# A fused attention and GLU kernel on one Trainium2 core: down and output projections of three blocks with the weights stationary

## The chip, the core and the metric

The kernel runs on one core of one Trainium2 chip. The core has a matrix engine (TensorE, PE in the profile; its weight loads are listed apart as PEld), three engines for elementwise work (VectorE or DVE, ScalarE or ACT, GpSimd or POOL) and DMA engines. SyncE (SP) issues most transfers; POOL issues those that accumulate. Every engine works through its own list of instructions in order, and waits at semaphores for the others. The metric is the time of one execution on the device in microseconds (us); less is better.

## What is computed

The input x has 2048 tokens of 640 features, in bf16. It is normalized over the features, and two branches read the result xn. The output is x plus both.

```python
xn = _layernorm(x)
# A: 32 heads of 20 features; each token sees 8 keys, at distances 0, 2, ..., 14
q, k, v = split(xn @ wqkv)
attn = softmax(mask(einsum("bhsd,bhswd->bhsw", q, kg) * scale))
A = einsum("bhsw,bhswd->bhsd", attn, vg) @ wo            # 640 -> 640
# B: gated linear unit, no activation function
h = (xn @ w_gate) * (xn @ w_up)                           # 640 -> 1536
B = h @ w_down                                            # 1536 -> 640
return x + A + B
```

## The kernel before

**Tiling.** The tokens are cut into 16 tiles of 128 and into 4 blocks (j = 0 to 3) of 512. Features lie in chunks of 128: 5 chunks (`NCH`) of the 640, 12 chunks (`NF`) of the 1536. PSUM has 8 banks of 128 x 512 fp32.

**A planner sets the order.** `Sched` (from L40) is no part of the chip's work. While the program is built, generators hand it tasks, each for one engine, with what it reads and writes, a priority (less is earlier), a number of PSUM banks and a `slack` by which it is thought to be ready later. The planner keeps a clock for each engine, advanced by the assumed cost of an instruction (`occ`; for an accumulating transfer `acc`), and emits the task that can start first. What it writes is one fixed list for each engine, with semaphore waits at every dependency. On the chip a list is never reordered: where an engine comes to an instruction whose input is late, it waits, and all that is behind it waits too.

**The stages.**
- `front(t)`: statistics, normalization and transposition of a tile into XNT (features on partitions). The first tiles are transposed on PE and copied out of PSUM; tiles 0 and 1 in two parts, chunks 0 and 1 and then 2 to 4, each on the engine that `COPY` names (L503; copies at L653 and L655). From tile 4 on a transposing transfer does it (L675, on SP's queue). PE runs 18 idle matmuls (`warm`, L680, L1531) before the first tile.
- `proj_qk`, `proj_v` (matmuls at L698 and L730): q, k and v.
- `products` and `logits`: products of q with shifted k on DVE (L880, L929). For blocks 2 and 3 (`QUAD`) fp32 products of five feature chunks are summed pairwise by POOL (L955, L966, L988) or by accumulating transfers that POOL issues (L951; `BY_DMA`). The sum of the fifth chunk (`name + "c"`, L966) is on POOL everywhere, since `LAST_DMA` is empty. PE sums over the features of a head with the matrix G (L1012).
- `softmax` (DVE and ACT), then `weighted`: 20 units u = 5j + c. In each, DVE multiplies the shifted values with the weights (L1191), POOL adds two halves (two adds a unit, L1196), and `sums` lets PE add up the rest with the matrix SEL (L1250), in batches of units that `BATCH` lists. ACT copies the batch into OT (L1259).
- `gu`: for block j and hidden chunk m, gate and up products on PE (L1314), ACT copies the gate, DVE multiplies with the up product (L1323), giving h. The pairs in `FAST` have up copied by ACT first, so that DVE multiplies from SBUF (L1361); such a multiply and a POOL operation exclude each other in the planner (`lock`).
- `dn(j)` with `dn_piece`: the down product and the output product accumulate into one bank. **Tokens are stationary**: for each of 4 token tiles and 2 halves of 320 features, 12 matmuls with `ht[:, rows]` as weights and WD as moving operand, then 5 with OT and WO (L1416, 320 columns each). The first 12 may be done ahead; the last 5 need OT, that is, the batch of `sums`. For j < 3 ACT copies the result to FB0 (L703), token tile by token tile, and after all eight POOL issues one transfer that adds FB0 to the output in HBM (L1442), where x was copied before. For j = 3 DVE adds x and SP stores.

**Banks around the end.** Two banks hold the softmax weights for `weighted`, each batch of `sums` wants a bank per unit at once, and a down product started before OT is there must leave that many free (`keep=next_sums`).

Of the kernel before, what the change touches and what calls it, by code (L numbers as in the profile page):

```python
# [49 lines left out]
class Sched:  # L50
# [78 lines left out]
    def op(self, eng, fn, r=(), w=(), dma=False, name="", occ=None, lat=None, lock=False, nbytes=0, mode=0, group=None, extra=0.0, acc=0.0, land=None):  # L129
# [19 lines left out]
        if dma:  # L149
            self.t[eng] = start + (0.48 if occ is None else occ)  # L150
            if acc:
                self.t_acc = max(self.t_acc, start + 3.8) + acc
                X.end = self.t_acc
            else:
                self.t_data = max(self.t_data, start + 1.2) + nbytes / 280e3
                X.end = self.t_data + 0.8 + extra
            if land is not None:
                X.end, self.t_data = land, max(land - 0.8, self.t_data - nbytes / 280e3)
        else:
            self.t[eng] = start + occ  # L160
            X.end = start + (occ if lat is None else lat)
# [194 lines left out]
def build_kernel(nc, A_x, A_wqkv, A_wo, B_x, B_w_gate, B_w_up, B_w_down, out):  # L356
# [65 lines left out]
    PRD += [sb("PRD12", [128, 4, JB], at=a_sc), sb("PRD13", [128, 4, JB], at=a_sc + 4096)]  # L422
    PRD32 = [K.sbuf(f"PRF{i}", [128, 2, JB], FP32, K.base[p.name]) for i, p in enumerate(PRD)]
    QUAD = {2: (1, 0), 3: (1, 0)}
    LAST_DMA = ()
    BY_DMA = (((0, 0), (0, 2)), ((1, 0), (1, 2)))
    a_xr = place[0]
    FB0 = sb("FB0", [128, 5, D])
# [71 lines left out]
    op("pool", lambda e: e.memset(KT[:, :, 0:PAD], 0.0), w=[KT[:, :, 0:PAD]], name="kpad", occ=0.3)  # L500

    PARTS = (((0, 2), (2, NCH)), ((0, 2), (2, NCH)))
    COPY = (("act", "act"), ("act", "dve"))  # L503

    def part_of(t, c):
        return next(k for k, (lo, hi) in enumerate(PARTS[t]) if lo <= c < hi)
# [170 lines left out]
            yield Task("sp", dmat, r=[xs], prio=1)  # L677
        mark("xnt", t)

    def warm(n):  # L680
        for _ in range(n):
            op("pe", lambda e: e.matmul(PS[:, 7, 0:QB], ZERO[:, 0:128], ZERO[:, 0:QB], start=True, stop=True),
               r=[ZERO[:]], w=[PS[:, 7, :]], name="warm", occ=0.2 if n > 3 else 0.12)

    def wcols(which, c, m):
        if which == 2:
# [77 lines left out]
    def proj_qk():  # L764
        for pair in (0, 2):
            for which in (0, 1):
                for t in (pair, pair + 1):
                    yield have("xnt", t)
                    K.spawn(proj_group([(which, 0, 4 if pair else 5)], t * TS, TS, 10 if pair else FIRST + 0.5 * which + 0.2 * t, None))
            if pair:  # L770
                for which in (0, 1):
                    K.spawn(proj_group([(which, 4, 1)], pair * TS, 2 * TS, 10.2, None))
        for t in (4, 6):
            yield have("xnt", t + 1)
            for items in ([(0, 0, 2)], [(1, 0, 2)], [(0, 2, 2)], [(1, 2, 2)], [(0, 4, 1), (1, 4, 1)]):
                K.spawn(proj_group(items, t * TS, 2 * TS, 11 + t * 0.1, None))
        for j in (2, 3):
            yield have("xnt", 4 * j + 3)
            for m in range(NCH):
                for which in (0, 1):  # L780
                    if which or j not in QUAD or m == NCH - 1:
                        K.spawn(proj_group([(which, m, 1)], j * JB, JB, 12 + j, None))
# [61 lines left out]

    def products():
        rows = {j: [] for j in range(NJ)}
        joined = []
        holds = {}
        for at, (j, kind) in enumerate(ORDER):
            if kind == "w":  # L850
                if j not in holds:
                    yield from fetch(j, 0, holds.setdefault(j, {c: [] for c in range(4)}))
                yield from wide(j, rows[j], holds[j])
            else:
                if len(QUAD.get(j, ())) == 2 and j not in holds and (j, "w") == ORDER[at + 1]:
                    yield from fetch(j, 0, holds.setdefault(j, {c: [] for c in range(4)}))
                for r in (1, 0):
                    for c in range(NCH - 1 if r in QUAD.get(j, ()) else 0, NCH):
                        yield from narrow(j, r, c, rows[j])
            if len(rows[j]) == 10 - 4 * len(QUAD.get(j, ())) and kind == ("w" if j in QUAD else "n"):  # L860
                if j in JOIN:
                    joined.append((j, rows[j]))
                    if len(joined) == len(JOIN):
                        K.spawn(logits(*joined))
                else:
                    K.spawn(logits((j, rows[j])))
        mark("products")

    def narrow(j, r, c, slots):
# [40 lines left out]
    def wide(j, slots, hold):  # L910
        halves = [(r, q0) for r in QUAD[j] for q0 in (0, 2)]
        acc, parts = {}, {1: [], 0: []}
        lastc = {r: [n, 0] for n, _, r in slots}
        slots.clear()
        for c0 in (0, 2):
            for i, (r, q0) in enumerate(halves):
                f = []
# [29 lines left out]
    def sum32(j, r, q0, p, a, b, last=None):  # L947
        x, y = PRD32[a][:], PRD32[b][:]
        name = f"qsum{j}_{r}_{q0}_{p}"
        if (r, q0) in BY_DMA[p]:  # L950
            yield Task("pool", lambda: op("pool", lambda e: e.dma_start(x, y, accum_op=ALU.add), r=[x, y], w=[x], dma=True,  # L951
                                          name=name, occ=0.88, acc=3.4), r=[x, y], w=[x], prio=4)
        else:
            yield calm
            yield Task("pool", lambda: op("pool", lambda e: e.tensor_tensor(x, x, y, ALU.add), r=[x, y] + tokens(), w=[x],  # L955
                                          name=name, occ=2.36, lock=True), r=[x, y], w=[x], prio=5, lock=True)
        free.append(b)
        if last is None:
            return
        z = PRD[last[0]][:, q0:q0 + 2, :]  # L960
        if (r, q0) in LAST_DMA:
            yield Task("pool", lambda: op("pool", lambda e: e.dma_start(x, z, accum_op=ALU.add), r=[x, z], w=[x], dma=True,
                                          name=name + "c", occ=0.88, acc=3.4), r=[x, z], w=[x], prio=4)
# [138 lines left out]
        yield Task("sp", move, r=[L[:]], prio=4)  # L1102

    NU = NJ * NCH
    BATCH = (4, 9, 14, 17, 19)

    def vx_loads():
        yield have("products")
# [42 lines left out]
    def unit(u):  # L1151
# [1 line left out]
        if c == 0:  # L1153
            yield have("atx", j // 2)
        yield have("vx", u)
        for k, (ok, n) in enumerate(((("atx", 1) in done, (9,)), (count.get(("dn", 0), 0) >= 8, (5,)),
                                     (count.get(("dn", 1), 0) >= 8, (6, 7, 8)))):
            if ok and k not in more:
                more.append(k)
                sv_free.extend(n)  # L1160
# [76 lines left out]
    def sums(us):  # L1237
# [1 line left out]
        for u in us:  # L1239
            yield have("add", u)  # L1240
        if us[-1] >= 3 * NCH:
            yield num(8, "dn", 2)

        def go(*bs):
            hold.extend(bs)
# [15 lines left out]
                K.free_bank(b, X)  # L1261
                bump("ot", j)

        yield Task("pe", go, r=[SV[sv_of[u]][:] for u in us], prio=9.7, banks=len(us), slack=0.7)
        yield Task("act", ev, r=[PS[:, b, :] for b in hold], prio=3)

    ucount = [0]
# [107 lines left out]
                mark("gu", j)  # L1375

    def xr_loads():
        yield num(8, "dn", 0)
# [8 lines left out]
    def dn(j):  # L1387
        yield num(NF, "h", j)
        if j:
            yield num(8, "dn", j - 1)  # L1390
        for st in range(4):
            t = 4 * j + st
            pieces = ((0, 256), (256, 512), (512, 640)) if t == NT - 1 else ((0, 320), (320, 640))
            if j == 3:
                yield have("xr", t)
            yield lambda: count.get(("ot", j), 0) >= NCH or ("gu", NJ - 1) in done
            for nb, (c0, c1) in enumerate(pieces):
                yield from dn_piece(j, t, nb, slice(st * TS, (st + 1) * TS), c0, c1)

    def dn_piece(j, t, nb, rows, c0, c1):  # L1400
        cols = slice(c0, c1)
        wid = c1 - c0
        hold = []
        n = NF + NCH
        F, ft = (FB1, t % 2) if j == 3 else (FB0, t % 4)
        o, xr = F[:, ft, cols], XR[:, t % 4, cols]

        def part(lo, hi):
# [21 lines left out]
                   name=f"fin{t}_{nb}", occ=0.15 + wid / 960)  # L1430
            K.free_bank(b, X)

        def fin_act():
            K.free_bank(hold[0], evac([(o, PS[:, hold[0], 0:wid], wid)], f"fin{t}_{nb}"))
            bump("fin", j)
            if count["fin", j] == 8:
                K.one(Task("pool", add_out, r=[F[:, 0:4, :]], prio=5))

        def add_out():
            d = ohbm[j * JB:(j + 1) * JB, :].rearrange("(t p) n -> p t n", p=128)  # L1440
            f = F[:, 0:4, :]
            stores.append(op("pool", lambda e: e.dma_start(d, f, accum_op=ALU.add), r=[f, ("outx",)], w=[("out", j)], dma=True,  # L1442
                             name=f"oadd{j}", occ=0.88, acc=4))

        def store():
            if t == NT - 1:
                f, d = o, ohbm[t * TS:(t + 1) * TS, cols]
# [4 lines left out]
        def tail():  # L1452
            yield num(NCH, "ot", j)
            yield Task("pe", rest, r=[OT[:, j, :, rows]], prio=40)
            if j < 3:
                yield Task("act", fin_act, r=[PS[:, hold[0], :]], w=[o], prio=6)
                return
# [6 lines left out]
        yield Task("pe", down, prio=41, banks=1, keep=0 if count.get(("ot", j), 0) >= NCH else next_sums, r=[WD[:], WO[:]])  # L1464
        K.spawn(tail())

    FAST = [(1, m) for m in range(6, NF)] + [(2, m) for m in range(4, 8)]
    JOIN = (2, 3)
    SLIP = 0.3
    N_PE_T = 4  # L1470
    BN_AFTER = (4,)
# [20 lines left out]
    x_load(2, land=9.0)  # L1492
    wqkv_load(1, 3, NCH, land=10.0)
    K.t["act"] = 2.1
    warm(18)

    def misc():
        yield have("xnt", NT - 1)
# [61 lines left out]
```

## Time and profile before

| | |
|---|---|
| median of 3 runs | 266.07 us (266.06 to 266.19) |
| the profiled execution's own time | 266.25 us |
| its span, first to last instruction | 264.4 us |
| instructions | 4405, of which 1748 matmuls |
| PE / DVE / POOL / ACT busy | 98% / 83% / 61% / 42% of the span |
| granted PE clock | 1.00 throughout |
| DMA | 37.83 MB, mean 143 GB/s |

The span lies inside the execution; 1.85 us of start and end lie around it. The page gives busy times, a strip of 40 slices of the span (a digit is the busy share of a slice in tenths), the chain of work that ended last, and groups of instructions by source line. A matmul's listed duration reaches from its issue to its modelled end and overlaps the next one, so rates are taken from the starts of a run of matmuls, as the chain of waits lists them (start, length, line, count), and not from the mean duration.

### The profile page before, as it was taken

What the parts mean: (1) busy time and instruction counts of PE and PEld (TensorE: products, weight loads), DVE (VectorE), ACT (ScalarE), POOL (GpSimd) and SP (SyncE); (2) the same over time, 40 slices, a digit from 0 to 9 for tenths busy, and PEclk for the clock granted to TensorE, in tenths of its full rate; (3) what the DMA queues carried; (4) which work ended last, traced back from release to release, by engine and by line L of the source; (5) the groups of instructions that cost most, each with busy time, mean ns of one, the idle gap of its engine ahead of it and who ended that gap; (6) DMA issues with size and microseconds to landing.
All of it is one profiled execution on the core that took longest, in us unless ns stands there. A gap on an engine that the chain in (4) does not pass through costs nothing.

```text
span 264.4 us, 4405 instructions
## 1 busy us (share of the span) xinstructions
PE 259.8 (98%) x1748; PEld 151.8 (57%) x1748; DVE 220.1 (83%) x259; ACT 111.9 (42%) x203; POOL 160.8 (61%) x97
## 2 busy tenths in 40 slices
PE   7999999999999999999999999999999999999996
PEld 4896975444444444444444444477646775776675
DVE  4787899999998799778779999999899998995032
ACT  3468987556612221224268652531235134213100
POOL 3000000000599998899973575599999999999300
DMA  6964679960379995470249425736586537600711
GB/s 207 373 211 84 126 95 383 443 233 18 121 136 187 234 222 111 85 144 1 61 132 308 90 47 121 152 86 157 153 166 138 147 93 124 129 1 0 102 50 50
DMA packets 39685, 37.83 MB, mean 143 GB/s; under 512 B 15697, under 2 KB 37329, under 8 KB 39633
## 3 DMA queue, kind: packets, MB, share of 16 engines
q1 hardware_dynamic: 36688, 31.32, 44.3%
q0 software_dynamic: 2736, 6.16, 13.5%
q8 instruction: 13, 0.21, 0.4%
q10 hardware_dynamic: 240, 0.07, 0.1%
q14 instruction: 8, 0.06, 0.1%
HBM read 25.07 MB, written 7.23 MB: 122 GB/s over the span
## 4 chain that ended last, share of the span: by engine, by line
PE 96%; DMA 2%; DVE 1%; SPq 0%; ACT 0%; issue 0%
PE PS L1314 39%; PE PS L1416 28%; PE PS L698 23%; PE PS L1012 2%; PE PS L1250 2%; PE PS L730 2%; DMA XST<-in_A_x_dram 2%; DVE STATS L574 0%; PE PS L642 0%; SPq L480 0%; ACT XNT L655 0%; DVE XNS L603 0%; ACT SD L584 0%; DVE FB L1429 0%; DVE MV L577 0%
## 5 line engine op out<-in xcount | busy, mean ns | idle before, releaser
L1196 POOL TENSOR_TENSOR SV<-PV 128x1024 bf16<-128x1024 f32 x40 | 94.4, 2384 | 17.1 <-DVE PV L1191 5.9
L1191 DVE TENSOR_TENSOR PV<-VX,PS 128x1024 f32<-128x1024 bf16 (+1 forms) x54 | 90.8, 1730 | 1.5 <-POOL SV L1196 1.5
L698 PE MATMUL PS<-XNT,WQKV 128*128 128x512 bf16 (+2 forms) x390 | 60.8, 316 | 0.0
L1314 PE MATMUL PS<-XNT,WG 128*128 128x512 bf16 x240 | 59.7, 379 | 0.0
L1314 PE MATMUL PS<-XNT,WU 128*128 128x512 bf16 x240 | 59.6, 379 | 0.0
L698 PEld LDWEIGHTS PS<-XNT,WQKV 128*128 128x128 bf16 x390 | 37.9, 112 | 21.9 <-ACT LOG L1023 0.8
L1314 PEld LDWEIGHTS PS<-XNT,WG 128*128 128x128 bf16 x240 | 23.2, 98 | 28.9 <-DVE XNT L1323 0.8
L1314 PEld LDWEIGHTS PS<-XNT,WU 128*128 128x128 bf16 x240 | 23.5, 98 | 28.0
L929 DVE TENSOR_TENSOR PRF<-PS,KT 128x1024 f32<-128x1024 f32 x32 | 37.9, 1218 | 0.3 <-PE PS L698 0.3
L955 POOL TENSOR_TENSOR PRF<-PRF,PRF 128x1024 f32<-128x1024 f32 x8 | 22.0, 2755 | 20.6 <-DVE LOG L1072 20.6
L703 ACT ACTIVATE HT<-PS 128x512 bf16<-128x512 f32 x24 | 14.3, 597 | 34.5 <-PE PS L1314 34.5
L1416 PE MATMUL PS<-WD,HT 128*128 128x320 bf16 x192 | 28.7, 299 | 0.0
L703 ACT ACTIVATE FB<-PS 128x320 bf16<-128x320 f32 x24 | 10.5, 437 | 40.4 <-PE PS L1416 40.4
L880 DVE TENSOR_TENSOR PRD<-QT,KT 128x2048 bf16<-128x2048 bf16 x24 | 27.3, 1222 | 0.0
L1031 POOL MEMSET LOG<- 32x6 bf16 (+6 forms) x7 | 0.4, 95 | 44.2 <-ACT LOG L1023 44.2
L1416 PE MATMUL PS<-WO,OT 128*128 128x320 bf16 (+2 forms) x165 | 26.5, 295 | 0.0
L1416 PEld LDWEIGHTS PS<-WD,HT 128*128 128x128 bf16 x192 | 18.8, 98 | 7.6
L988 POOL TENSOR_TENSOR PRD<-PRF,PRF 128x1024 bf16<-128x1024 f32 x8 | 21.5, 2768 | 0.1
L966 POOL TENSOR_TENSOR PRF<-PRF,PRD 128x1024 f32<-128x1024 f32 x8 | 19.5, 2543 | 0.0
L1416 PEld LDWEIGHTS PS<-WO,OT 128*128 128x128 bf16 x165 | 16.0, 98 | 5.8
L1323 DVE TENSOR_TENSOR HT<-HT,PS 128x512 bf16<-128x512 bf16 x18 | 12.3, 686 | 7.0 <-PE PS L1314 7.0
L1429 DVE TENSOR_TENSOR FB<-PS,XR 128x320 bf16<-128x320 f32 (+2 forms) x9 | 4.1, 454 | 16.5 <-PE PS L1416 16.5
(72 smaller groups left out, 247.1 us busy)
## 6 DMA issues: line engine op xcount, KB each, us to landing
VX<-v_scratch SPq DMA_DIRECT2D x80, 130.0 KB, 3.1
PRF<-PRF POOLq DMA_DIRECT2D x8, 512.0 KB, 5.1
XST<-in_A_x_dram SPq DMA_DIRECT2D x16, 160.0 KB, 5.4
v_scratch<-VST SPq DMA_DIRECT2D x4, 640.0 KB, 6.5
WG<-in_B_w_gate_dram SPq DMA_DIRECT2D x1, 1920.0 KB, 8.8
WU<-in_B_w_up_dram SPq DMA_DIRECT2D x1, 1920.0 KB, 12.2
out_dram<-in_A_x_dram SPq DMA_DIRECT2D x1, 1920.0 KB, 19.7
WD<-in_B_w_down_dram SPq DMA_DIRECT2D x1, 1920.0 KB, 8.2
```

What stands on the lines that cost most here:

```text
L698: op("pe", (lambda o, l, x, c, first: lambda e: e.matmul(o, l, x, start=first, stop=(c == NCH - 1)))(o, l, x, c, first), r=[l, x], w=[o], ...
L703: X = op("act", (lambda o, i: lambda e: e.activation(o, i, ACT.Copy))(o, i), r=[i], w=[o], name=name, occ=0.12 + n * 0.9e-3)
L880: op("dve", lambda e: e.tensor_tensor(s[:], qb, kv, ALU.mult), r=[q, rk], w=[s[:]], name=f"prod{j}_{r}_{c}", occ=1.15, lock=True)
L929: X = op("dve", lambda e: e.tensor_tensor(o[:], qb, kv, ALU.mult), r=[q, rk, ("qev", j, c)], w=[o[:]], name=f"prow{j}_{r}_{c}_{q0}", occ=1.17)
L955: yield Task("pool", lambda: op("pool", lambda e: e.tensor_tensor(x, x, y, ALU.add), r=[x, y] + tokens(), w=[x], name=name, occ=2.36, lock ...
L966: yield Task("pool", lambda: op("pool", lambda e: e.tensor_tensor(x, x, z, ALU.add), r=[x, z] + tokens(), w=[x], name=name + "c", occ=2.36 ...
L988: yield Task("pool", lambda: op("pool", lambda e: e.tensor_tensor(o, a, y, ALU.add), r=[a, y] + tokens(), w=[o], name=f"qend{j}_{r}_{q0}", ...
L1191: last[0] = op("dve", lambda e: e.tensor_tensor(p, vw, a, ALU.mult), r=[vv] + rk, w=[p], name=f"pv{u}_{x}_{r0}", occ=0.09 + 1.1 * nr)
L1196: X = op("pool", lambda e: e.tensor_tensor(o, p[:, :, 0, :], p[:, :, 1, :], ALU.add), r=[p[:]] + tokens(), w=[o], name=f"pva{u}_{x}", occ= ...
L1314: op("pe", (lambda l, x, c: lambda e: e.matmul(PS[:, b, :], l, x, start=(c == 0), stop=(c == NCH - 1)))(l, x, c), r=[l, x], w=[PS[:, b, :] ...
L1323: X = op("dve", lambda e: e.tensor_tensor(h, h, PS[:, hold[1], :], ALU.mult), r=[h, PS[:, hold[1], :]], w=[h], name=f"h{m}_{j}", occ=0.65)
L1416: op("pe", (lambda l, x, i: lambda e: e.matmul(dst, l, x, start=(i == 0), stop=(i == n - 1)))(l, x, i), r=[l, x], w=[PS[:, b, :]], name=f" ...
```

## The change

1. **`dn` for blocks 0 to 2 goes by feature columns (`dn_cols`).** For each of five chunks of 128 output features, 12 matmuls with a 128 x 128 piece of WD as weights and the 512 tokens of h as moving operand, then 5 with WO and OT. The result has features on partitions. ACT copies it to one of three buffers UX (128 x 512, bf16), and SP issues a transposing transfer from UX to the columns of FB0 (15 of them). After the fifth of a block POOL issues the accumulating transfer as before. Block 3 stays as it was.
2. **`BATCH`** joins the last two batches: units 15 to 19 in one. **`slack`** of `sums` goes from 0.7 to 4.0, so that all four batches are put later in PE's list.
3. **`LAST_DMA`**: four sums of the fifth chunk (two in block 2, two in block 3) go from POOL to accumulating transfers that POOL issues.
4. **`FAST`** takes in the pairs (3, 0) to (3, 3).
5. **`COPY[1]`**: the two copies of tile 1 swap engines. **`warm`**: 9 matmuls of 512 columns in place of 18 of 256.
6. The planner's assumptions: an accumulating transfer starts 1.6 after its issue and not 3.8, and takes 3.1 in place of 3.4 (4.6 in place of 4 for the one to the output).

Further edits (`JOIN` as a tuple of groups, conditions on `QUAD` and `rows`) give the same program with the values set here.

```diff
-                self.t_acc = max(self.t_acc, start + 3.8) + acc
+                self.t_acc = max(self.t_acc, start + 1.6) + acc
...
-    LAST_DMA = ()
+    LAST_DMA = ((1, 2), (0, 2))
...
-    COPY = (("act", "act"), ("act", "dve"))
+    COPY = (("act", "act"), ("dve", "act"))
...
-    BATCH = (4, 9, 14, 17, 19)
+    BATCH = (4, 9, 14, 19)
...
-        yield Task("pe", go, r=[SV[sv_of[u]][:] for u in us], prio=9.7, banks=len(us), slack=0.7)
+        yield Task("pe", go, r=[SV[sv_of[u]][:] for u in us], prio=9.7, banks=len(us), slack=4.0)
...
+        if j < 3:
+            for c in range(NCH):
+                yield lambda: count.get(("ot", j), 0) >= NCH or ("gu", NJ - 1) in done
+                yield from dn_cols(j, c)
+            return
...
+    def dn_cols(j, c):
+        cols = slice(c * 128, (c + 1) * 128)
+        hold = []
+        n = NF + NCH
+        k = (j * NCH + c) % NUX
+        y, o = UX[:, k, :], FB0[:, 0:4, cols]
+
+        def part(lo, hi):
+            b = hold[0]
+            for i in range(lo, hi):
+                l, x = (WD[:, i, cols], ht(j, i)) if i < NF else (WO[:, i - NF, cols], OT[:, j, i - NF, :])
+                op("pe", (lambda l, x, i: lambda e: e.matmul(PS[:, b, :], l, x, start=(i == 0), stop=(i == n - 1)))(l, x, i),
+                   r=[l, x], w=[PS[:, b, :]], name=f"do{j}_{c}_{i}", occ=0.2158, lat=0.3)
...
+        def ev():
+            K.free_bank(hold[0], evac([(y, PS[:, hold[0], :], JB)], f"doev{j}_{c}"))
+
+        def turn():
+            op("sp", lambda e: e.dma_start_transpose(o, y), r=[y], w=[o], dma=True, name=f"dot{j}_{c}", nbytes=160e3, occ=1.0, extra=1.3)
+            bump("fin", j)
+            if count["fin", j] == NCH:
+                K.one(Task("pool", add_out, r=[FB0[:, 0:4, :]], prio=5))
...
-    FAST = [(1, m) for m in range(6, NF)] + [(2, m) for m in range(4, 8)]
-    JOIN = (2, 3)
+    FAST = [(1, m) for m in range(6, NF)] + [(2, m) for m in range(4, 8)] + [(3, m) for m in range(4)]
+    JOIN = ((2, 3),)
...
-    warm(18)
+    warm(9, JB)
```

More of the change, by code (lines that the diff above doesn't have):

```diff
@@ L678, in front, with warm @@
         mark("xnt", t)
-    def warm(n):
+    def warm(n, cols=QB):
         for _ in range(n):
-            op("pe", lambda e: e.matmul(PS[:, 7, 0:QB], ZERO[:, 0:128], ZERO[:, 0:QB], start=True, stop=True),
-               r=[ZERO[:]], w=[PS[:, 7, :]], name="warm", occ=0.2 if n > 3 else 0.12)
+            op("pe", lambda e: e.matmul(PS[:, 7, 0:cols], ZERO[:, 0:128], ZERO[:, 0:cols], start=True, stop=True),
+               r=[ZERO[:]], w=[PS[:, 7, :]], name="warm", occ=0.4 if cols > QB else 0.12)
     def wcols(which, c, m):
@@ L775, in proj_qk @@
             for items in ([(0, 0, 2)], [(1, 0, 2)], [(0, 2, 2)], [(1, 2, 2)], [(0, 4, 1), (1, 4, 1)]):
-                K.spawn(proj_group(items, t * TS, 2 * TS, 11 + t * 0.1, None))
+                if 1 not in QUAD or items[0][0] or items[0][1] == 4:
+                    K.spawn(proj_group(items, t * TS, 2 * TS, 11 + t * 0.1, None))
         for j in (2, 3):
@@ L846, in products @@
         rows = {j: [] for j in range(NJ)}
-        joined = []
+        joined = {}
         holds = {}
@@ L857, in products @@
                 for r in (1, 0):
+                    if (r in QUAD.get(j, (r,) if kind == "n" else ())) != (kind == "n"):
+                        continue
                     for c in range(NCH - 1 if r in QUAD.get(j, ()) else 0, NCH):
                         yield from narrow(j, r, c, rows[j])
[L860 to L866, printed above, removed]
+            if len(rows[j]) == 10 - 4 * len(QUAD.get(j, ())) and kind == ("n" if j not in QUAD else "w" if len(QUAD[j]) > 1 else "m"):
+                group = next((g for g in JOIN if j in g), (j,))
+                joined[group] = joined.get(group, ()) + ((j, rows[j]),)
+                if len(joined[group]) == len(group):
+                    K.spawn(logits(*joined[group]))
         mark("products")
@@ L912, in wide @@
         acc, parts = {}, {1: [], 0: []}
-        lastc = {r: [n, 0] for n, _, r in slots}
-        slots.clear()
+        lastc = {r: [n, 0] for n, _, r in slots if r in QUAD[j]}
+        slots[:] = [e for e in slots if e[2] not in QUAD[j]]
         for c0 in (0, 2):
@@ L951, in sum32 @@
             yield Task("pool", lambda: op("pool", lambda e: e.dma_start(x, y, accum_op=ALU.add), r=[x, y], w=[x], dma=True,
-                                          name=name, occ=0.88, acc=3.4), r=[x, y], w=[x], prio=4)
+                                          name=name, occ=0.88, acc=3.1), r=[x, y], w=[x], prio=4)
         else:
@@ L962, in sum32 @@
             yield Task("pool", lambda: op("pool", lambda e: e.dma_start(x, z, accum_op=ALU.add), r=[x, z], w=[x], dma=True,
-                                          name=name + "c", occ=0.88, acc=3.4), r=[x, z], w=[x], prio=4)
+                                          name=name + "c", occ=0.88, acc=3.1), r=[x, z], w=[x], prio=4)
         else:
@@ L1155, in unit @@
         yield have("vx", u)
-        for k, (ok, n) in enumerate(((("atx", 1) in done, (9,)), (count.get(("dn", 0), 0) >= 8, (5,)),
-                                     (count.get(("dn", 1), 0) >= 8, (6, 7, 8)))):
+        for k, (ok, n) in enumerate(((("atx", 1) in done, (9,)), (count.get(("dn", 0), 0) >= NCH, (5,)),
+                                     (count.get(("dn", 1), 0) >= NCH, (6, 7, 8)))):
             if ok and k not in more:
@@ L1241, in sums @@
         if us[-1] >= 3 * NCH:
-            yield num(8, "dn", 2)
+            yield num(NCH, "dn", 2)
         def go(*bs):
@@ L1377, in xr_loads @@
     def xr_loads():
-        yield num(8, "dn", 0)
+        yield num(NCH, "dn", 0)
         for st in range(4):
@@ L1389, in dn @@
         if j:
-            yield num(8, "dn", j - 1)
+            yield num(NCH, "dn", j - 1)
+        if j < 3:
[3 more added lines that the diff above has]
+            return
         for st in range(4):
@@ L1393, in dn @@
             pieces = ((0, 256), (256, 512), (512, 640)) if t == NT - 1 else ((0, 320), (320, 640))
-            if j == 3:
-                yield have("xr", t)
+            yield have("xr", t)
             yield lambda: count.get(("ot", j), 0) >= NCH or ("gu", NJ - 1) in done
@@ L1398, in dn, with down, rest, add_out @@
                 yield from dn_piece(j, t, nb, slice(st * TS, (st + 1) * TS), c0, c1)
+    def dn_cols(j, c):
[10 more added lines that the diff above has]
+                   r=[l, x], w=[PS[:, b, :]], name=f"do{j}_{c}_{i}", occ=0.2158, lat=0.3)
+        def down(b):
+            hold.append(b)
+            part(0, NF)
+        def rest():
+            part(NF, n)
+            bump("dn", j)
+        def ev():
[5 more added lines that the diff above has]
+                K.one(Task("pool", add_out, r=[FB0[:, 0:4, :]], prio=5))
+        def add_out():
+            d = ohbm[j * JB:(j + 1) * JB, :].rearrange("(t p) n -> p t n", p=128)
+            f = FB0[:, 0:4, :]
+            stores.append(op("pool", lambda e: e.dma_start(d, f, accum_op=ALU.add), r=[f, ("outx",)], w=[("out", j)], dma=True,
+                             name=f"oadd{j}", occ=0.88, acc=4.6))
+        def tail():
+            yield num(NCH, "ot", j)
+            yield Task("pe", rest, r=[OT[:, j]], prio=40)
+            yield Task("act", ev, r=[PS[:, hold[0], :]], w=[y], prio=6)
+            yield Task("sp", turn, r=[y], w=[o], prio=5)
+        yield Task("pe", down, prio=41, banks=1, keep=0 if count.get(("ot", j), 0) >= NCH else next_sums, r=[WD[:], WO[:]])
+        K.spawn(tail())
     def dn_piece(j, t, nb, rows, c0, c1):
@@ L1404, in dn_piece @@
         n = NF + NCH
-        F, ft = (FB1, t % 2) if j == 3 else (FB0, t % 4)
+        F, ft = FB1, t % 2
         o, xr = F[:, ft, cols], XR[:, t % 4, cols]
@@ L1431, in fin @@
             K.free_bank(b, X)
[L1433 to L1443, printed above, removed]
         def store():
@@ L1454, in tail @@
             yield Task("pe", rest, r=[OT[:, j, :, rows]], prio=40)
-            if j < 3:
-                yield Task("act", fin_act, r=[PS[:, hold[0], :]], w=[o], prio=6)
-                return
             yield Task("dve", fin, r=[PS[:, hold[0], :], xr], w=[o], prio=FIN_PRIO)
```

## The prediction

> **What bounds the kernel now.** I read the page's head and its strip, then the chain of work that ended last in order of time, then the starts of single matmuls, then the last 45 us of each engine.
>
> ```profile
> span 264.4 us, 4405 instructions
> PE 259.8 (98%) x1748; PEld 151.8 (57%) x1748; DVE 220.1 (83%) x259; ACT 111.9 (42%) x203; POOL 160.8 (61%) x97
> ...
> PE   7999999999999999999999999999999999999996
> ```
>
> PE is busy in every slice but the first and the last. A busy PE may still be one that waits within a modelled duration, so the starts decide. From 8.74 to 262.15 the chain never leaves PE:
>
> ```profile
> 74.86 16.19 PE PS L1314 x75
> ...
> 172.21 18.47 PE PS L1416 x136
> ...
> 200.62 18.47 PE PS L1416 x136
> 219.09 3.24 PE PS L1314 x15
> 222.33 1.19 PE PS L1250 x20
> 223.52 18.58 PE PS L1416 x136
> 242.10 0.76 PE PS L1250 x12
> 242.86 5.00 PE PS L1416 x36
> 247.86 0.55 PE PS L1250 x8
> 248.40 13.75 PE PS L1416 x117
> ```
>
> The columns are start, length, line and count. L1416 at 320 columns goes at 18.47 / 136 = 0.1358 us a matmul, L1314 at 512 columns at 16.19 / 75 = 0.2159 us. Against these rates the single starts show, between 8.74 and the end, no gap over 0.04 us except where PE changes between full and 32-column stationary matrices: 0.09 us ahead of each group at L1012 or L1250 and 0.10 us behind it. So PE's list of columns, one after the other, is the time. Nothing that only frees DVE, ACT or POOL can gain, and every wait that PE gets costs its full length.
>
> The second bound is close. From 171.84 POOL does the adds of L1196 almost without a pause, and the last of them decides when the last batch of sums can run:
>
> ```profile
> 222.12 21.09 POOL L1196 TENSOR_TENSOR SV<-PV 128x1024 bf16<-128x1024 f32 x9 [0.53 <-DVE PV L1191]
> ...
> 243.14 1.29 POOL L1442 DMA_DIRECT2D out_dram<-FB  x1
> 243.96 2.86 POOL L1196 TENSOR_TENSOR SV<-PV 128x1024 bf16<-128x1024 f32 x1
> ```
>
> The last add ends at 246.82, and PE starts the sums that need it at 247.79: 0.97 us to spare, of which 0.09 is the change of matrix.
>
> **Part 1, down and output by columns.** Three blocks x 136 matmuls x 320 columns are 130,560 columns; three x 85 x 512 are 130,560 as well. What goes is only the fixed part of 51 matmuls a block. A block costs 85 x 0.2159 = 18.35 us in place of 18.47: 0.12 us less, **0.36 us** over three blocks. All of it is on the path. Weight loads fall from 136 to 85, but at 98 ns each they lie beside matmuls of 136 or 216 ns already and pay nothing.
>
> One rule would make far more of this. The Trainium skill, "TensorE: Matmul & The Clock Gate", section "Back-to-back issue gap", gives N/2.4 + 2.5 ns as the gap of isolated matmuls and about 131 ns as the sustained spacing at 512 columns in streams of weight load and matmul. By the 131 ns an estimate for three blocks is 33 us, 22 less than now. The row here is such a stream, and it takes 215.9 ns; the measurement decides.
>
> ACT's copies: 24 of 437 ns go (10.5 us), 15 of 597 ns come (9.0 us). Each comes every 3.67 us and is needed by nobody before its transfer.
>
> The transposing transfer is new at this place. The nearest row is XNT<-XNS, five 128 x 128 tiles where this has four: SP is held 1.2 to 1.4 us (once 2.3), and it lands 2.6 to 4.2 us after issue. The cost on PE's path is bounded by zero and by what a late one holds up: a buffer is wanted again after 3 x 3.67 = 11.0 us, less 0.6 for the copy, so even 4.2 us is hidden. Below zero it can't go, since no PE instruction reads FB0. I take zero. The price if the cover goes stands under the rivals. SP has room: 15 x 1.3 = 20 us in some 75 us, in which it mostly waits for DVE (72.9 us at 15 waits over the whole span).
>
> The Trainium skill, "VectorE: DVE Perf Modes", section "The three transpose paths", speaks against this transfer: 1309 ns for one 128 x 128 by DMA, 390 ns on TensorE. Four of these in a row are 5.2 us, an estimate by that page; the row above has five tiles in 2.6 us. At 5.2 us it would still fit into the 10.4 us, and the sum stays.
>
> **Part 2, the batches.** Groups of 12 and 8 sums cost 0.77 (242.03 to 242.80) and 0.55 us (247.79 to 248.34), with 0.09 ahead of each: 1.50. One of 20 costs 1.19 (222.26 to 223.45) + 0.09 = 1.28. **0.22 us** go, on the path. The added wait: units 15 to 17 are now copied to OT only after unit 19's add. Behind the batch stand the output matmuls of block 3. Ahead of it PE has only three down products, as now: with two banks held and five kept, or with those two free again, 8 - 5 = 3. PE therefore comes to the batch at 247.69 - 0.36 - 0.86 (the group of 12 and its change) = 246.5. The last add must end by then. It ended at 246.82, but the transfer at 243.14 stood before it (add 9 of the run ends at 243.21, an add takes 2.34 us: 245.6 without it). Behind the batch, five copies take 2.56 us (L1259 at 222.71), and the next down product (1.63 us) starts when the first of them has freed a bank, during the sums. The longer slack for the first three batches moves gate and up matmuls ahead of them: after 169.76 there are 60 of these left, 13.0 us, so PE isn't short. Buffers SV: units 10 to 14 and 15, 16 fill seven, the eighth comes with the end of block 1, ahead of unit 17. Zero.
>
> **Part 3, four sums on transfers.** POOL loses 4 x 2.33 us and gets four issues; after an issue the next add starts 0.6 to 0.8 us later (100.89 to 101.50, 73.72 to 74.48). Some 6.5 us of POOL go between 74 and 123. Such a transfer lands 4.5 to 7.5 us after issue (eight of them, median 5.1), so of the 6.5 I expect 2 to 5 to arrive at the end of the product stage (POOL ends there at 132.60). PE gains nothing from it. But the logits of blocks 2 and 3 at 134.15 come exactly where the 260 gate and up matmuls that may run ahead of them are used up, so they mustn't come later. Taken: zero on PE, 2 to 4 us earlier for the chain of adds.
>
> **Part 4, four more fast multiplies.** DVE: 4 x (686 - 424) = 1.05 us less. ACT: 4 x 597 = 2.4 us more at 42% busy. POOL must stand still for each; it has 0.6 to 2.7 us of idle time between its adds from 154 to 172, where these fall. Zero on PE.
>
> **Part 5, the start.** PE waits from the transposes of tile 1 at 8.04 to 8.74:
>
> ```profile
> 8.30 0.38 ACT L655 ACTIVATE XNT<-PS 128x256 bf16<-128x256 bf16 x1 [0.96 <-PE PS L642]
> 8.58 0.70 ACT L703 ACTIVATE QT<-PS 128x640 bf16<-128x640 f32 x1
> 8.65 0.36 DVE L653 COPY XNT<-PS 128x384 bf16<-128x384 bf16 x1 [0.44 <-PE PS L642]
> 8.73 2.84 PEld L730 LDWEIGHTS PS<-XNT,WQKV 128*128 128x128 bf16 x50 [0.30 <-ACT XNT L655]
> ```
>
> The first part will be copied by DVE, free at 8.21. Its copies take 0.36 us for 384 and 0.49 for 640 columns, so 0.29 for 256, against 0.38 on ACT: **0.09 us**. The second part on ACT takes 0.49 (its row of 384), until 9.12; PE has ten matmuls of 0.056 us from 8.65, until 9.21. It fits by 0.05 us after the semaphore. Bounds: zero, if tiles 2 and 3 (XNS ready 0.1 to 0.5 us ahead of PE) are then what PE waits for, and 0.1. I take 0.09, since DVE moves up as well. The warm matmuls have the same columns and end before PE's wait at 4.7 to 5.42: zero.
>
> **The sum.** 0.36 + 0.22 + 0.09 = 0.67 us. The profiled execution took 266.25 (span 264.4), so it becomes 265.58; against the median, 0.18 lower, 266.07 - 0.67 = **265.4 us**. Worked bounds without new waits: 265.3 to 265.5.
>
> **Rivals.**
>
> *A short wait of PE eats part of it.* Two places are near: the logits of blocks 2 and 3, if the chain of two transfers in a row lands 1 to 3 us later than the planner's 4.7 us (measured up to 7.5), against a slack of 2.0; and the last batch, if POOL's transfer for block 2 still stands before the last add (246.8 against 246.5, with 0.1 for the semaphore 0.4 us). For it: both margins are under 2 us. Against: POOL gains time. 0.2 to 1.2 us of wait give 265.6 to 266.6; middle 266.0.
>
> *Slower: POOL is held by the fifth transfer of a block.* POOL's transfer to the output (L1442) now waits in POOL's list for a transfer on SP's list, where VX loads stand that wait for DVE, one group each 4.4 to 5.2 us (172.92, 177.31, 181.71, 186.10). If the fifth stands behind one, POOL stands still for up to one such period, with the later adds of L1196 behind it, and the last batch comes late. The margin is 246.5 - 245.6 = 0.9 us, and 2 to 4 more if part 3 works. A hold of 4.4 us in two blocks, with 8.8 - 0.9 - 4 = 3.9 us left, gives 269.3; one hold with 2 us won earlier, 4.4 - 2.9 = 1.5, gives 266.9. It decides the sign from 0.67 us of wait on, the 0.2% from 1.2 on. Against it: the planner puts SP's list in order of expected start, and PE has run on time.
>
> *The change doesn't do what it says.* Columns don't fall, so a reader who hopes for less PE work finds 0.36 us; if the batch and the start gave nothing, 265.7.
>
> **Chances.** Forecast 0.58; short wait 0.20; held POOL 0.17 (266.9 the likelier end); only the 0.36 us 0.05. About 0.2%, 0.53 us, is what a measurement here can tell from no change: 265.54 and 266.60 are the bounds. The forecast's case lies under 265.54; of the short waits a few are under it, most within. Faster 0.60, same 0.22, slower 0.18. The range takes the forecast's low bound, 265.3, less 0.1 for a start that moves further and 0.1 for the spread of the runs: 265.1; at the top one held POOL, 266.9.
>
> **What would show it.** Right: L1416 in runs of 85 at 18.35 us, one group of 20 ahead of block 3, PE's first projection of tile 1 at 8.65, no gap over 0.04 us elsewhere, POOL's last add under 246.5. Wrong: a gap of PE ahead of L1012 near 134 or of L1250 near 246, a POOL wait for FB0, a PE start later than 8.74.

## The result and the profile after

The changed kernel takes 267.82 us (median of 15 runs, 266.67 to 271.03), the kernel before in the same comparison 266.19 (15 runs, 265.79 to 267.19). The ratio is 1.0059, with a 95% interval of 1.0038 to 1.0081: slower by 1.6 us, where 0.67 us less was forecast. The profiled execution took 267.85 us. From the page of the kernel after, the head, PE's strip and the row of one kind of transfer (count, KB each, median us from issue to landing):

```profile
span 266.1 us, 4096 instructions
...
PE 260.4 (98%) x1586; PEld 136.3 (51%) x1586; DVE 218.2 (82%) x259; ACT 111.6 (42%) x198; POOL 156.1 (59%) x97
...
PE   8999999999999999999999999699999999999996
...
PRF<-PRF POOLq DMA_DIRECT2D x8, 512.0 KB, 7.3
```

PE now has one slice of 6 in the middle of its nines, the 26th, which is 166.3 to 173.0 us. The last line says where to look next: the accumulating transfers land a median 7.3 us after issue; before it was 5.1. In the kernel after, these lines stand one further down than before (L1251 is before's L1250, L1315 is L1314, L1197 is L1196, L930 is L929); L1416 is now `dn_cols`, and block 3's output matmuls are L1467. The chain of waits of the kernel after, in order of time, around that slice and from there to the end:

```profile
168.29 2.37 POOL SV L1197
...
170.76 0.06 DVE XNT L1362
...
171.10 0.69 DVE XNT L1324
171.83 0.40 PE PS L1251 x4
172.23 1.19 PE PS L1315 x5
173.42 18.35 PE PS L1416 x85
...
200.62 18.35 PE PS L1416 x85
...
225.55 18.45 PE PS L1416 x85
244.00 4.89 PE PS L1467 x36
248.90 1.19 PE PS L1251 x20
250.09 13.75 PE PS L1467 x117
```

Two things are to be seen. The lower half is what the prediction drew: 85 matmuls in 18.35 us and one group of 20 ahead of block 3. The upper half isn't: before, the chain stayed on PE; now it leaves PE and runs over POOL and DVE until 171.83. PE's timeline of the kernel after there (start, us, operation, in brackets the idle time ahead and what ended it):

```profile
168.77 1.05 PE L1251 MATMUL PS<-SV,SEL 128*32 128x512 bf16 x16
171.83 0.40 PE L1251 MATMUL PS<-SV,SEL 128*32 128x512 bf16 x4 [2.01 <-DVE XNT L1324]
```

The same batch before:

```profile
169.76 1.26 PE L1250 MATMUL PS<-SV,SEL 128*32 128x512 bf16 x20
170.96 1.25 PE L1314 MATMUL PS<-XNT,WG 128*128 128x512 bf16 x5
```

In the first batch of sums PE gets four banks, does 16 sums and waits 2.01 us for the fifth, which a multiply of `gu` on DVE has to free. From its start to the start of what follows, the batch takes 3.40 us (168.77 to 172.17) in place of 1.19 (169.76 to 170.96).

**The account.** The stretch from the start of the first transpose of tile 1 to the start of the last matmul leaves out the kernel's start, which moves with the landing of x. It was 253.94 us before and is 255.57 after: +1.63, the whole of the difference. The longer batch is +2.21 (3.40 - 1.19), so about 0.6 us were won elsewhere: nearly the forecast's 0.67.

**Where DVE got late.** Of the idle times that ended in a transfer, the longest of DVE is at 108.48. DVE's timeline, first after, then before:

```profile
104.12 0.69 DVE L1324 TENSOR_TENSOR HT<-HT,PS 128x512 bf16<-128x512 bf16 x1 [0.67 <-PE PS L1315]
108.48 1.22 DVE L930 TENSOR_TENSOR PRF<-PS,KT 128x1024 f32<-128x1024 f32 x1 [3.67 <-DMA PRF<-PRF]
```

```profile
101.10 3.48 DVE L929 TENSOR_TENSOR PRF<-PS,KT 128x1024 f32<-128x1024 f32 x3
104.49 0.68 DVE L1323 TENSOR_TENSOR HT<-HT,PS 128x512 bf16<-128x512 bf16 x1
```

A product of block 3 writes a PRF buffer that an accumulating transfer still reads. Both kernels issue that transfer at 100.9; before, it lands at 105.40 (4.51 us), after, at 108.45 (7.55). The order of the lists assumed 1.6 + 3.1 = 4.7 and put the product at the planned landing itself, 104.60, with no margin; before, the same product goes at 103.36, as the last of the three in the first line of the second view, and waits for nothing. From the DMA part of both traces, 100 to 112 us (packets, MB, share of 16 engines), after and then before:

```profile
q0 software_dynamic: 429, 1.56, 62.1%
q1 hardware_dynamic: 840, 0.77, 33.8%
```

```profile
q0 software_dynamic: 293, 1.07, 47.0%
q1 hardware_dynamic: 27, 0.02, 0.8%
```

The transfers that POOL issues are q0; q1 carries SP's. After, the first 16 loads of VX run beside the transfer (the last lands at 105.39); before, the last of them had landed by 101.26. They slipped because the store of v ahead of them did: 86.94 to 96.08 in place of 84.68 to 92.82, with two added transfers of block 2 (issued 74.47 and 85.71, landed 81.12 and 93.69) in front of it and beside it.

Against the times that the planner gives its instructions while the program is built, DVE is 0.98 us late ahead of that product and 3.87 us after it. It wins back only 1 us and loses it again before the first batch: 2.85 us at the subtraction of the softmax, 4.28 at the multiply that PE waits for. In the kernel before it is never more than 1.3 us late.

**Theory A** is this chain: part 3's transfers delay the loads, the loads delay an accumulating transfer, the list was ordered for an early landing, DVE waits, and PE pays 60 us later. **A1** adds that block 2's two transfers do it, not block 3's. **The rival B**: part 4. The four new fast multiplies exclude POOL's adds and have two buffers UF. DVE's timeline of the kernel after shows them with waits in between (the wait ahead of 170.76 ends, by the chain above, with POOL's add of 168.29):

```profile
167.79 0.42 DVE L1362 TENSOR_TENSOR XNT<-XNT,UF 128x512 bf16<-128x512 bf16 x1 [0.33 <-ACT UF L703]
168.13 1.21 DVE L1192 TENSOR_TENSOR PV<-VX,PS 128x1024 f32<-128x1024 bf16 x1
170.76 0.42 DVE L1362 TENSOR_TENSOR XNT<-XNT,ZERO 128x512 bf16<-128x512 bf16 x1 [1.41 <-ACT OT L1260]
171.10 0.68 DVE L1324 TENSOR_TENSOR XNT<-XNT,PS 128x512 bf16<-128x512 bf16 x1
```

### The profile page after: what moved, and what is told of

Same layout as the page of the kernel before. It is cut to its first block, busy times and chain, and to the rows that moved or that the text cites. A ratio compares the mean times of both kernels' runs of the same rounds, so it can differ in the third digit from the quotient of the medians.

```text
span 266.1 us, 4096 instructions
## 1 busy us (share of the span) xinstructions
PE 260.4 (98%) x1586; PEld 136.3 (51%) x1586; DVE 218.2 (82%) x259; ACT 111.6 (42%) x198; POOL 156.1 (59%) x97
## 4 chain that ended last, share of the span: by engine, by line
PE 85%; DVE 7%; POOL 5%; ACT 1%; issue 1%; DVEq 0%
PE PS L1315 26%; PE PS L698 23%; PE PS L1416 21%; PE PS L1467 7%; POOL SV L1197 5%; PE PS L730 2%; DVE PV L1192 2%; PE PS L1013 2%; PE PS L682 2%; PE PS L1251 1%; DVE SM L1046 1%; DVE HT L1362 1%; DVE HX L1362 1%; PE PS L642 1%; DVE OT L1324 0%
## 5 line engine op out<-in xcount | busy, mean ns | idle before, releaser
L1197 POOL TENSOR_TENSOR SV<-PV 128x1024 bf16<-128x1024 f32 x40 | 94.3, 2482 | 17.3 <-DVE HT L1362 8.8
L1315 PE MATMUL PS<-XNT,WG 128*128 128x512 bf16 x240 | 59.7, 379 | 0.0
L1315 PE MATMUL PS<-XNT,WU 128*128 128x512 bf16 x240 | 59.6, 379 | 0.0
L930 DVE TENSOR_TENSOR PRF<-PS,KT 128x1024 f32<-128x1024 f32 x32 | 37.9, 1215 | 4.6 <-DMA PRF<-PRF 4.6
L1315 PEld LDWEIGHTS PS<-XNT,WG 128*128 128x128 bf16 x240 | 23.3, 98 | 28.7 <-ACT LOG L1024 0.4
L1315 PEld LDWEIGHTS PS<-XNT,WU 128*128 128x128 bf16 x240 | 23.4, 98 | 28.3 <-issue 0.2
L956 POOL TENSOR_TENSOR PRF<-PRF,PRF 128x1024 f32<-128x1024 f32 x8 | 19.3, 2425 | 20.8 <-DVE LOG L1073 20.6
L1416 PE MATMUL PS<-HT,WD 128*128 128x512 bf16 x120 | 27.5, 379 | 0.0
L703 ACT ACTIVATE UX<-PS 128x512 bf16<-128x512 f32 x15 | 9.0, 597 | 42.3 <-PE PS L1416 42.3
L989 POOL TENSOR_TENSOR PRD<-PRF,PRF 128x1024 bf16<-128x1024 f32 x8 | 19.0, 2404 | 0.2
L1416 PEld LDWEIGHTS PS<-HT,WD 128*128 128x128 bf16 x120 | 11.8, 98 | 14.1
L1416 PE MATMUL PS<-OT,WO 128*128 128x512 bf16 x75 | 18.6, 379 | 0.0
L574 DVE BATCH_NORM_STATS2 STATS<-XST 128x6 f32<-128x320 bf16 x32 | 14.0, 470 | 3.5 <-DMA XST<-in_A_x_dram 3.5
L703 ACT ACTIVATE VST<-PS 128x512 bf16<-128x512 f32 x20 | 11.7, 592 | 6.3 <-PE PS L698 6.2
```

Source lines behind the costliest of these rows:

```text
L574: op("dve", lambda e: e.bn_stats(o, a), r=[a], w=[("st", t, i)], name=f"bn{t}_{i}", occ=0.49)
L703: X = op("act", (lambda o, i: lambda e: e.activation(o, i, ACT.Copy))(o, i), r=[i], w=[o], name=name, occ=0.12 + n * 0.9e-3)
L930: X = op("dve", lambda e: e.tensor_tensor(o[:], qb, kv, ALU.mult), r=[q, rk, ("qev", j, c)], w=[o[:]], name=f"prow{j}_{r}_{c}_{q0}", occ=1.17)
L1197: X = op("pool", lambda e: e.tensor_tensor(o, p[:, :, 0, :], p[:, :, 1, :], ALU.add), r=[p[:]] + tokens(), w=[o], name=f"pva{u}_{x}", occ= ...
L1315: op("pe", (lambda l, x, c: lambda e: e.matmul(PS[:, b, :], l, x, start=(c == 0), stop=(c == NCH - 1)))(l, x, c), r=[l, x], w=[PS[:, b, :] ...
L1416: op("pe", (lambda l, x, i: lambda e: e.matmul(PS[:, b, :], l, x, start=(i == 0), stop=(i == n - 1)))(l, x, i), r=[l, x], w=[PS[:, b, :]], ...
```

## The experiments

Each was compared with the kernel before on the same chip. "Stretch" is that of the account; before 253.94, after 255.57.

**vx_late.** The kernel after, with the first loads of VX made to wait for the product that follows the late one (block 3, row group 1, chunk 3). The lists that the planner writes for the five engines have the same instructions in the same order as in the kernel after; only this wait is new.

```diff
-  r=[q, rk, ("qev", j, c)], w=[o[:]],
+  r=[q, rk, ("qev", j, c)], w=[o[:]] + ([("vxgo",)] if (j, r, c, q0) == (3, 1, 3, 0) else []),
...
-                rk = [("vscr", "pad")] + ...
+                rk = [("vxgo",), ("vscr", "pad")] + ...
```

> The changed kernel, with one wait added: the first 16 VX loads wait for the DVE product of block 3, row group 1, chunk 3, so that they no longer share the DMA engines with the accumulating transfers between 88 and 105 us. Theory A (the four added transfers land 2 to 3 us later than the planner assumes, DVE waits for a buffer at 104.8 and stays some 4 us late until 171, where PE waits 2.0 us inside the first batch of sums for a bank that a late multiply holds): the transfers issued near 101 and 104 land after 4.5 to 6 us instead of 7.1 to 7.6, DVE's wait falls from 3.7 us to under 1.5, PE's wait in the first batch falls under 0.5, time 265.4 to 266.4. Rival B (the four added fast multiplies, which must alternate with POOL's adds, make DVE late): nothing changes, 267.3 to 268.2. Rival C (transposing transfers and three buffers UX cost the time): nothing changes, 267.3 to 268.2.

Measured: 265.44 us (10 runs), ratio 0.9971 [0.9958, 0.9985], stretch 253.43. The transfer lands 4.55 us after issue (100.53 to 105.08). In its DMA part for 100 to 112 us q1 has 5.3% and not 33.8%, and DVE's timeline has

```profile
105.11 1.23 DVE L930 TENSOR_TENSOR PRF<-PS,KT 128x1024 f32<-128x1024 f32 x1 [0.68 <-DMA PRF<-PRF]
```

PE's first batch is nearly undisturbed, 1.39 us in place of 3.40:

```profile
168.32 1.45 PE L1251 MATMUL PS<-SV,SEL 128*32 128x512 bf16 x20
169.71 1.25 PE L1315 MATMUL PS<-XNT,WU 128*128 128x512 bf16 x5
```

The whole loss goes with a change that takes no work away, reorders nothing and leaves part 4 in place. The loads now start at 108.09 and meet later accumulating transfers, of which the slowest lands 10.58 us after issue (112.34 to 122.92); DVE is then at most 2.3 us late, and PE pays nothing more than the 0.2 us of this batch. So it matters which transfer is late.

**no_fast3.** The kernel after without part 4.

```diff
-    FAST = [(1, m) for m in range(6, NF)] + [(2, m) for m in range(4, 8)] + [(3, m) for m in range(4)]
+    FAST = [(1, m) for m in range(6, NF)] + [(2, m) for m in range(4, 8)]
```

> The changed kernel without its part 4: the pairs (3, 0) to (3, 3) multiply from PSUM as before. Theory A: DVE still waits 3 to 4 us for a landing near 105 and is still some 4 us late at 165; the bank that the first batch waits for is still released late, time 266.6 to 268. Rival B: PE's wait in the first batch is gone, 265.4 to 265.8. Rival C: 267.3 to 268.2.

Measured: 266.38 us (12), 1.0005 [0.9995, 1.0016], stretch 254.32. From its waits (us in total, times, longest):

```profile
DVE PRF L930 <- DMA PRF<-PRF: 4.6, 2, 3.7
...
PE PS L1251 <- DVE XNT L1324: 0.8, 1, 0.8
```

Only DVE's and ACT's lists change. DVE waits for the late transfer as before, and PE still waits for the fifth bank, 0.78 us in place of 2.01. So part 4 alone isn't the cause, but here it makes the wait 1.2 us longer. The time lies below A's range and above B's. DVE's lateness falls from 3.83 to 3.24 us over these multiplies without the fast ones; with them it rises from 3.84 to 4.28.

**cols_only.** The kernel before with part 1 alone (`dn_cols`).

> The kernel before with part 1 alone: blocks 0 to 2 by feature columns with the 15 transposing transfers, and the planner's 4.6 for the transfer to the output; batches, slack, LAST_DMA, FAST, COPY and the other assumptions as before. Theories A and B: 0.36 us less than the kernel before, 265.6 to 266.0, no wait of PE. Rival C: slower than before by 0.4 or more, with PE gaps near the end of blocks 0 to 2 or POOL waits for FB0.

Measured: 265.63 us (12), 0.9982 [0.9973, 0.9990], stretch 253.60: 0.34 less than before, where the prediction gave the columns 0.36. PE has no new wait, so rival C of the expectations (the transposing transfers cost the time) falls.

**no_last_dma.** The kernel after without part 3.

```diff
-    LAST_DMA = ((1, 2), (0, 2))
+    LAST_DMA = ()
```

> The changed kernel without its part 3: the four sums of the fifth chunk are on POOL again, the planner's assumptions stay at 1.6 and 3.1. Theory A: accumulating transfers land after 4.5 to 5.5 us in block 3, DVE's wait for a landing falls under 1 us, PE's wait in the first batch falls under 0.5; POOL has 6.5 us more to do before its adds, which may cost at the last batch; time 265.5 to 266.5. Rival B: PE waits in the first batch as now, 267 to 268. Rival C: 267 to 268.

Measured: 266.26 us (12), 1.0003 [0.9994, 1.0012], stretch 254.25. DVE's wait is 0.8 us and the first batch runs through. But about 1.0 us of new gaps appears behind the third batch (up to 227.8), which the next runs explain.

**cols_batch_copy.** The kernel before with part 1, the joined batch of part 2 at the old slack of 0.7, and part 5.

> The changed kernel without parts 3 and 4, with slack 0.7 and the old 3.8 and 3.4 for accumulating transfers: what is left is the columns (part 1), the joined last batch of part 2, and part 5. Theory A: nothing makes DVE late, no PE wait in or behind a batch, so the three gains of the prediction come as summed, 0.36 + 0.22 + 0.09: 265.3 to 265.6. Rival (the joined batch or the swapped copies cost something of their own): 265.7 or more, with a PE gap at 247 or at 8.7.

Measured: 265.22 us (6), 0.9962 [0.9944, 0.9980], stretch 253.25: 0.69 less than before. From its chain:

```profile
218.41 3.24 PE PS L1315 x15
221.65 1.19 PE PS L1251 x20
222.84 18.45 PE PS L1416 x85
241.29 4.89 PE PS L1467 x36
246.18 1.19 PE PS L1251 x20
```

PE is without a gap here. This is the forecast's sum (0.67), and the lowest median of all kernels measured; its interval overlaps those of vx_late and block3_transfers.

**acc_old.** The kernel after with the planner's old assumptions. No work changes, only the order of the lists.

```diff
-                self.t_acc = max(self.t_acc, start + 1.6) + acc
+                self.t_acc = max(self.t_acc, start + 3.8) + acc
...
- occ=0.88, acc=3.1
+ occ=0.88, acc=3.4
```

> The changed kernel with the planner's old assumptions for accumulating transfers alone (start 3.8, 3.4 each, 4 to the output): the four transfers of part 3 stay. Theory A: the planner no longer puts a DVE product ahead whose buffer comes free only after 7 us, so DVE's longest wait for a landing falls under 1 us and PE's wait in the first batch under 0.5; the adds are then not earlier, and the slack of 4.0 leaves PE short of work behind the third batch, 1 to 1.5 us: time 266.0 to 266.8. Rival (the transfers themselves cost the time, whatever is assumed): 267.3 to 268.2.

Measured: 266.66 us (12), 1.0018 [1.0009, 1.0028], stretch 254.64. Neither DVE nor the first batch waits, although all transfers of part 3 are there. What is left over cols_batch_copy, 1.39 us of stretch, lies in two other places: about 1.0 us of gaps behind the third batch (226.4 to 227.8), and 0.4 us inside the logits at 134.8, where PE waits for a copy of ACT. The run doesn't show that allowing for a late landing is what helps: the new order issues the first transfer of block 3 only at 105.40, when the last load has landed (105.41), and it takes 4.55 us.

**transfers_only.** The kernel before with parts 3 and 6.

> The kernel before with parts 3 and 6 alone (four sums on transfers, start 1.6 and 3.1 assumed). Theory A: transfers of block 3 land after 6 to 7.5 us, DVE waits 2 to 4 us for one and is 3 to 4 us late at 165; with direct multiplies and a slack of 0.7 PE waits for the first batch or a bank, 0.5 to 2 us: 266.5 to 268. Rival B (the fast multiplies are needed for a loss): no PE wait, 265.9 to 266.3.

Measured: 268.67 us (6), 1.0093 [1.0075, 1.0110], stretch 256.26. The transfer takes 7.63 us, DVE waits 3.7, and PE's timeline around the first batch shows

```profile
165.35 0.83 PE L1250 MATMUL PS<-SV,SEL 128*32 128x512 bf16 x12
166.99 0.62 PE L1250 MATMUL PS<-SV,SEL 128*32 128x512 bf16 x8 [0.81 <-DVE XNT L1323]
168.72 1.25 PE L1314 MATMUL PS<-XNT,WG 128*128 128x512 bf16 x5 [1.12 <-DVE XNT L1323]
```

There is no fast multiply of (3, 0) to (3, 3) in this kernel, and PE waits 1.93 us: B falls as the cause. The stretch is 2.32 us longer than before, more than A expected. That this and the 0.69 of cols_batch_copy add up to +1.63, just what the change made, is in part luck: part 4 and the longer slack are in neither run, and the wait is at another point of another list.

**batch_slack_only.** The kernel before with part 2.

> The kernel before with part 2 alone: the joined last batch and the slack of 4.0. If the slack needs the earlier adds of part 3: the output matmuls of block 2 come right behind the third batch and wait for ACT's copies one by one, 1.2 to 1.8 us, less 0.22 for the joined batch: 267.0 to 267.8. If the slack is free, as the prediction had it: 265.8 to 266.0.

Measured: 267.30 us (6), 1.0043 [1.0028, 1.0058], stretch 255.04. PE's timeline behind the third batch:

```profile
223.54 1.26 PE L1250 MATMUL PS<-SV,SEL 128*32 128x512 bf16 x20
224.74 0.71 PE L1416 MATMUL PS<-WO,OT 128*128 128x320 bf16 x2
225.62 0.31 PE L1416 MATMUL PS<-WO,OT 128*128 128x320 bf16 x1 [0.18 <-ACT OT L1259]
226.12 0.31 PE L1416 MATMUL PS<-WO,OT 128*128 128x320 bf16 x1 [0.18 <-ACT OT L1259]
226.61 0.31 PE L1416 MATMUL PS<-WO,OT 128*128 128x320 bf16 x1 [0.18 <-ACT OT L1259]
```

A matmul of 320 columns takes 0.136 us; these follow each other at 0.5 us. Before, two down products (24 matmuls, 223.45 to 226.72) stood between this batch and the first output matmul. With the slack the batch comes later in the list, behind a down product, and PE goes straight on to the output matmuls, each of which wants a chunk of OT that ACT is just copying. This costs 0.26 + 3 x 0.36 = 1.33 us, and no_last_dma and acc_old show the same place. In the kernel after it doesn't occur: there the group behind that batch takes 18.45 us, 0.10 over the others.

**block2_transfers, block3_transfers.** The kernel after, with part 3 in one block only.

```diff
-        if (r, q0) in LAST_DMA:
+        if (r, q0) in LAST_DMA and j == 2:
```

(`j == 3` in the second.)

> The changed kernel with the added transfers in block 2 alone (issued near 74.5 and 85.7); in block 3 the two sums of the fifth chunk are on POOL. Theory A1 (the two of block 2 fill the DMA engines between 74 and 94, the moves of the weights, the store of v and the first VX loads slip by some 2 to 3 us, and the first transfer of block 3 meets them): the first transfer of block 3, near 101, lands after 7 us or more, DVE waits 3 us or more for it, PE waits 0.5 to 2 us near 170: 266.4 to 268. Theory A2 (it is the density of block 3's own transfers): it lands after 4.5 to 5.5 us, no PE wait, 265.4 to 265.9.

> The changed kernel with the added transfers in block 3 alone (issued after 104); in block 2 the two sums are on POOL. Theory A1: the first transfer of block 3 lands after 4.5 to 5.5 us, DVE's wait for it is under 1 us, no PE wait near 170: 265.4 to 265.9. Theory A2: it lands after 6 us or more or a later one does, DVE waits 2 to 4 us, PE waits 0.5 to 2 us near 170: 266.4 to 268.

Measured: block 2 alone 265.79 us (12), 0.9986 [0.9971, 1.0000], stretch 254.08; block 3 alone 265.39 us (11), 0.9963 [0.9952, 0.9974], stretch 253.24. The line of the product in DVE's timeline, with block 2's and then with block 3's transfers:

```profile
108.18 1.23 DVE L930 TENSOR_TENSOR PRF<-PS,KT 128x1024 f32<-128x1024 f32 x1 [3.85 <-DMA PRF<-PRF]
```

```profile
103.52 1.23 DVE L930 TENSOR_TENSOR PRF<-PS,KT 128x1024 f32<-128x1024 f32 x1 [0.82 <-DMA PRF<-PRF]
```

A1 holds for the landing: 7.74 us with block 2's, where the first 16 loads land until 105.05, and 5.14 with block 3's, where they land until 100.86. For the time it doesn't hold: 265.79 lies in the range of its rival A2, because with the full landing delay PE's wait is only 0.65 us (at 170.78). Taking out either pair brings back 2.0 to 2.4 us of the changed kernel's 267.82. Both runs have other lists than the kernel after, so how much of a DVE delay reaches PE depends on what else was planned in between, and that part of A isn't quantitative.

## Why the prediction was wrong

**The step that failed is part 3: "Taken: zero on PE, 2 to 4 us earlier for the chain of adds."** Its second half came: in POOL's timeline the adds of L1197 begin at 130.13 and not at 132.57, the logits on PE at 129.84 and not 134.15. The first half, zero on PE, did not. The step asked only what POOL and the logits gain. It never asked who waits for a buffer that an accumulating transfer releases (DVE, L930), nor which transfers the added 2 MB would push behind them. The row was in hand, "4.5 to 7.5 us after issue"; its upper end against the planner's new 4.7 was carried to the logits alone. The step cost 2.32 us (transfers_only, with part 6), or 2.2 us of PE's first batch in the kernel after, where part 4 has a share of 1.2. None of the signs of being wrong that the prediction named looked at the first batch.

**Part 6 has no term in the sum at all**, and part 3 didn't cost this alone. With part 3 and the old assumptions (acc_old), and with the new assumptions and no part 3 (no_last_dma), DVE's wait for a landing stays under 1 us and the first batch isn't held up; only together do they put the transfer among the loads while the product stands at the planned landing.

**Part 4, "Zero on PE"**, was wrong in this company. Taken out of the kernel after, 1.2 us of the wait go; in vx_late, where DVE is less late, it costs no more than the 0.2 us by which the first batch is longer.

**Part 2.** The 0.22 us came: a batch of 20 costs 1.19 us, and cols_batch_copy is 0.35 us of stretch shorter than cols_only, where the batch and the start together were to give 0.31. The longer slack, "Zero", asked whether PE has work ahead of the batch and not what stands behind it. Alone it costs 1.33 us; in the changed kernel 0.10, so this mistake didn't decide.

**Parts 1 and 5** held. L1416 goes at 18.35 us for 85; ACT has 15 copies of 597 ns; the 15 transposing transfers hold SP 1.2 to 1.3 us each and mostly land 2.4 to 3.1 us after issue (once 5.08), and PE waits for none. From the first transpose of tile 1 to the first projection it was 0.76 us with the old copies and is 0.66 to 0.67 in all eight kernels with the new ones, 0.09 as worked out. The timeline of the kernel after shows how: ACT's part ends behind DVE's, covered by PE's ten matmuls.

```profile
8.34 0.29 DVE L653 COPY XNT<-PS 128x256 bf16<-128x256 bf16 x1 [0.17 <-PE PS L642]
8.61 0.49 ACT L655 ACTIVATE XNT<-PS 128x384 bf16<-128x384 bf16 x1 [1.30 <-PE PS L642]
8.69 3.39 PEld L730 LDWEIGHTS PS<-XNT,WQKV 128*128 128x128 bf16 x60 [0.29 <-DVE XNT L653]
```

Of the two rules that were weighed in these steps, the first didn't hold here, and the estimate from the second was too long. By the 131 ns of the Trainium skill ("TensorE: Matmul & The Clock Gate", "Back-to-back issue gap") 22 us would have gone, and 0.34 went. By its 1309 ns for a 128 x 128 transpose by DMA ("VectorE: DVE Perf Modes", "The three transpose paths") four tiles would be 5.2 us, an estimate; they mostly took 2.4 to 3.1.

**The rivals.** "A short wait of PE eats part of it" named the right source, late accumulating transfers, but the wrong waiter and place, and 0.2 to 1.2 us where it was 2.2. "POOL is held" came true as a wait and cost nothing: from POOL's timeline of the kernel after,

```profile
238.65 4.65 POOL L1197 TENSOR_TENSOR SV<-PV 128x1024 bf16<-128x1024 f32 x2 [0.17 <-DVE PV L1192]
247.36 1.30 POOL L1439 DMA_DIRECT2D out_dram<-FB  x1 [4.06 <-DMA FB<-UX]
```

POOL stands 4.06 us for the fifth transfer, but behind the last add (ended 243.30), with nothing in its list that PE still needs.

**What stays open.** The runs of the changed kernel spread over 266.67 to 271.03, those of cols_batch_copy over 265.11 to 265.67; why the first spread so far was not followed up. And vx_late moves the loads in time, so it shows that loads beside the transfer slow it, not by which resource of the DMA engines. Why the same delay of DVE costs PE 2.2 us in the kernel after and 0.65 in block2_transfers was not traced through the lists.

## What to carry to other kernels

Where the order is fixed beforehand, a moved piece of work is to be priced at everyone who waits for its buffers, and the assumed duration that the order is built on is to be checked against the whole spread of the row, not its best: acc_old took this wait away with other assumptions alone, though by issuing the transfer after the loads and not by allowing for a long landing. Moving work from a busy engine to DMA is not free because the engine gains: list the transfers that follow in the next 30 us, and what each of them releases. A delay of an engine off the path can reach the path 60 us later, at the next place where all banks are wanted at once.

## What the runs showed of the hardware

- The same accumulating transfer of 512 KB, issued at the same time, landed after 4.51 us (q1 at 0.8% in that window) and after 7.55 us (33.8%, loads of 130 KB each); with the loads moved away, 4.55. In block3_transfers, issued at 98.36 with loads landing until 100.86, it took 5.14.
- A transposing transfer of four 128 x 128 tiles from SBUF to SBUF mostly landed 2.4 to 3.1 us after issue (once 5.08), shorter than the five-tile row of the kernel before (2.6 to 4.2).
- Streams of weight load and matmul ran at 215.9 ns a matmul for 512 columns and 135.8 for 320, at a granted clock of 1.00: in proportion to the columns but for about 1 ns.
